# Attention and gated MLP on one core: the order of TensorE's products, by array shape, in the attention passes

## The chip, the cores and the metric

The kernel runs on one core of one Trainium2 chip. The metric is device time in microseconds (us) of one execution; lower is better. For the kernel before there are three timed runs and one profiled execution.

## What is computed

```python
scores = scale * np.matmul(q, k.transpose(0, 1, 3, 2))     # batch 4, 12 heads, 448 rows, head_dim 64
scores = cap * np.tanh(scores / cap)
scores = scores - np.max(scores, axis=-1, keepdims=True)
attn = np.exp(scores)
attn = attn / (np.sum(attn, axis=-1, keepdims=True) + 1e-09)
x = np.matmul(attn, v)                                      # laid out as (1792, 768)
h = x @ w_in                                                # w_in 768 x 2048
g = h * (1.0 / (1.0 + np.exp(-h)))
return (g @ w_out).astype(np.float32)                       # w_out 2048 x 768
```

## The kernel before, in words

The program has two stages, `attention()` and `moe()`. The change touches the first.

A head pair is two heads of one batch, one in partitions 0 to 63, the other in 64 to 127. Attention works through 24 pairs, two in a pass, so there are 12 passes. The order of all engines' work in a pass is written out by hand in the table `SLOT`: `attention()` reads its words from left to right and calls `step()` on each, and every engine keeps the order in which its instructions were recorded. In a word, `i` and `k` name the first and the second pair of the pass, the digit names a chunk of 128 keys, `r` the 64 keys that are left of 448 (of both pairs together), and `+1`, `-1`, `-2`, `-4` another pass. Two tables in `ENDS` stand in for `SLOT` in the last pass and after it.

The words, and what they record:

- `Q` (`qk`, L318; `Qr` is `qk_rem`, L330) is the scores of one chunk, keys by rows. TensorE's array is used in four quarters of 64x64: four products of 64 keys and 448 rows, which run side by side. This is one *group*; the profile shows every product twice, so a group is 8 records. It goes to one of three score tiles `s` in PSUM.
- `T` (`tanh`, L340; `Tr` is L344) is ScalarE's tanh out of the score tile into `P` in SBUF, which gives the score tile free. `E` (`exp`, L348) is the exponential in place in `P`: one over 1792 columns for chunks 0 and 1, one over 896 for chunk 2, one over 896 for the rest.
- `V` (`pv`, L380) multiplies `P` with the values `VT`: products of shape 128x64, two side by side, 4 records a group. `Vr` (`pv_rem`, L388) does so for the rest, in the 64x64 shape. All add up in one PSUM tile `o`, of which there is one; `UC` (`u_vals`, L409) copies it out on VectorE before the next pass may write it.
- `S` (`sums`, L358, L363) adds `P` up over key chunks on VectorE into `T`; `A` (`fold`, L392) adds the rest by two accumulating DMAs from GpSimd's queue; `SUM` (`pv_sum`, L402) multiplies `T` with ones (shape 128x32, one group) into a score tile, and `UT` and `N` turn the sums round, send them through the `R` DMAs and scale `U` with them.
- `L1` loads the keys and queries `QK` of pair 2s+3 and the values `VT` of the next pass, in each third pass the `VB` of the rest too; `L2` loads `QK` of pair 2s+4. There are three `QK` tiles, so each load waits for the last product that reads the tile. All these are issued by GpSimd, one after the other. `D1` and `D2` decode 64-bit weights on VectorE (`decode`), by the table `FIRST`; the last step of a weight's decoding lets GpSimd load the next raw weight into `RAW` (L603, L605), three times in the passes.
- `H` in the last two passes are six parts of the first MLP product (128x128).

So a pass has 15 groups on TensorE: seven of Q and one of Vr in the shape 64x64, six of V in 128x64, and one of SUM in 128x32.

Of the kernel before, what the change touches and what calls it, by code (L numbers as in the profile page):

```python
# [185 lines left out]
def tile_softcap_attention_swish_moe(  # L186
# [18 lines left out]
    S = NT // B  # L205
    D = DM // (2 * NP)
    KC = S // 128
# [37 lines left out]
    VT = [a1.tile([128, 2, 2 * KC * D], F32, name=f"VT{r}") for r in range(2)]  # L245
# [49 lines left out]
    def scores_tile():  # L295
        return ps_s.tile([128, 2, 512], F32, tag="s", name="s")

    def load_rem(b, eng=nc.gpsimd):
        v = vrem[b].rearrange("k (u t) d -> k u t d", t=2)
        for t in range(2):  # L300
            for e in range(2):
                eng.dma_start(out=VB[b % 2][half(t), :, e], in_=v[half(e), :, t, D * e:D * e + D])

    def load_qk(i, eng=nc.gpsimd, c0=0, c1=S + KW):
        eng.dma_start(out=QK[i % 3][:, c0:c1], in_=qkv[i, :, c0:c1])  # L305

    def load_v(s, eng=nc.gpsimd):
        for t in range(2):
            eng.dma_start(out=VT[s % 2][:, t], in_=qkv[2 * s + t, :, S + KW:])

    def qk(i, j):

        q = QK[i % 3]
        ps = scores_tile()
        for c in range(2):
            for e in range(2):
                k0 = S + 128 * j + 64 * c
                nc.tensor.matmul(  # L318
                    ps[half(c), e, 0:S], q[half(e), k0:k0 + 64], q[half(e), 0:S], start=True, stop=True
                )  # L320
        SP[i, j] = ps
# [24 lines left out]
    def exp(i, h):  # L346
        p = P[i, h]
        nc.scalar.activation(out=p, in_=p, func=AF.Exp, scale=factor(capt))  # L348

    def flat(t):  # L350
        return t.rearrange("p a s -> p (a s)")

    def sums(i, n):
# [8 lines left out]
        else:  # L362
            nc.vector.tensor_tensor(flat(T[i]), flat(T[i]), flat(p), ALU.add)  # L363

    DONE = {}

    def summed(i):
        if i // 2 not in O:
            O[i // 2] = ps_o.tile([128, 2, 512], F32, tag="o", name="o")
        n = DONE[i] = DONE.get(i, 0) + 1  # L370
        return n == 1, n == KC + 1

    def pv(i, j):

        s, t = divmod(i, 2)
        start, stop = summed(i)
        for e in range(2):
            v = VT[s % 2][:, t, D * (e * KC + j):D * (e * KC + j) + D]
            p = P[i, j // 2][:, 2 * (j % 2) + e]
            nc.tensor.matmul(O[s][half(e), t, 0:S], v, p, start=start, stop=stop)  # L380

# [8 lines left out]
    def fold(s):  # L390
        for t in range(2):
            nc.gpsimd.dma_start(out=T[2 * s + t][half(t)], in_=P[s, "r"][half(t)], accum_op=ALU.add)  # L392

    def pv_sum(s, folded=True):

        ps = scores_tile()
        for z in (1,) if folded else (0, 1):
            for t in range(2):
                for e in range(2):
                    k = 2 * e + t  # L400
                    a, p = (1 + t, P[s, "r"]) if z == 0 else (0, T[2 * s + t])
                    nc.tensor.matmul(  # L402
                        ps[32 * k:32 * k + 32, 0, 0:S], ones[:, a], p[:, e], start=(z == 0 or folded), stop=(z == 1)
                    )
        US[s] = ps

    def u_vals(s):
        U[s] = au.tile([128, 2, S], F32, tag="U", name="U", bufs=3)
        nc.vector.tensor_copy(U[s], O.pop(s)[:, :, 0:S])  # L409
# [4 lines left out]
    def u_sums(s, parts=(0, 1, 2)):  # L414
        if 0 in parts:
            UW[s] = au.tile([128, S // 32, 32], F32, tag="US", name="US", bufs=2)
            nc.vector.transpose(flat(UW[s]), US.pop(s)[:, 0, 0:S])
        if 1 in parts:
            CW[s] = au.tile([128, S // 32], F32, tag="CS", name="CS", bufs=1)
            nc.vector.reciprocal(out=CW[s], in_=UW[s][:, :, 0])  # L420
        if 2 not in parts:
            return
        u = UW.pop(s)
        nc.vector.transpose(u, CW.pop(s).unsqueeze(2).to_broadcast([128, S // 32, 32]))
        rt = flat(u)

        r = au.tile([128, 2, S], F32, tag="R", name="R", bufs=2)
        for e in range(2):
            for h in range(2):
                for c in range(2):  # L430
                    nc.sync.dma_start(
                        out=r[64 * e + 32 * h:64 * e + 32 * h + 32, c], in_=rt[64 * e + 32 * c:64 * e + 32 * c + 32]
                    )
        RB[s] = r

    def norm(s, parts=(0, 1, 2)):
        b, u = s // NU, s % NU
        cs = slice(b * S, (b + 1) * S)
        x = U[s]
        xh, xl = XH[:, 2 * u:2 * u + 2, cs], XL[:, 2 * u:2 * u + 2, cs]  # L440
        if 0 in parts:
            nc.vector.tensor_tensor(flat(x), flat(x), flat(RB.pop(s)), ALU.mult)
        if 1 in parts:
            nc.vector.tensor_copy(xh, x)
        if 2 in parts:
            nc.vector.tensor_tensor(xl, x, xh.bitcast(F32), ALU.subtract)
            if s == NS - 1:
                tail.close()
                MPOOL["acc2"] = pool(core, "acc2", 1, side="right")
# [36 lines left out]
    }  # L486

    SLOT = """
        Ti0 N0-4 Vk1-1 Ti1 Vk0-1 Sk1-1 Er-1 SUM-2 Ti2 N1-4 Vk2-1 A-1 UT0-2 Ei0 Vr-1 N2-4 Qr Ei1 UT1-2 Qk0 UC-1 L1 Tr Qk1
        Si0 Tk0 Qk2 Tk1 D1 Qi0+1 L2 Tk2 D2 Vi0 Ek0 UT2-2 Vi2 Si1 Vi1 Qi1+1 Ek1 Sk0 Qi2+1  # L490
    """.split()

    ENDS = {
        NS - 1: """
        Ti0 N0-4 Vk1-1 Ti1 Vk0-1 Sk1-1 Er-1 SUM-2 Ti2 N1-4 Vk2-1 A-1 UT0-2 Ei0 Vr-1 N2-4 Qr Ei1 UT1-2 Qk0 UC-1 Tr Qk1
        Si0 Tk0 Qk2 Tk1 D1 H0 Tk2 Vi0 Ek0 UT2-2 Vi2 Si1 Vi1 H1 Ek1 Sk0 H2
        """.split(),
        NS: """
        N0-4 Vk1-1 Vk0-1 Sk1-1 Er-1 SUM-2 N1-4 Vk2-1 Vr-1 N2-4 UC-1 H3 H4 H5 UT0-2 UT1-2 UT2-2 SUM-1 UT0-1 UT1-1 UT2-1
        """.split(),  # L500
    }

    def step(op, sh, slot):
        s = slot + sh
        if not 0 <= s < NS:
            return
        i = 2 * s + (1 if op[1:2] == "k" else 0)
        j = int(op[2]) if op[2:3].isdigit() else None
        if op == "SUM":
            pv_sum(s, s + 1 < NS)  # L510
        elif op == "UC":
            u_vals(s)
        elif op[:2] == "UT":
            u_sums(s, (j,))
        elif op[0] == "N":
            norm(s, (int(op[1]),))
        elif op[0] == "D":
            if (slot, op) in FIRST:
                decode(*FIRST[slot, op])
        elif op == "A":  # L520
            if s + 1 < NS:
                fold(s)
        elif op == "L1":
            if s + 1 < NS:
                load_qk(2 * s + 3)
                load_v(s + 1)
                if (s + 1) % NU == 0:
                    load_rem((s + 1) // NU)
        elif op == "L2":
            if s + 2 < NS:  # L530
                load_qk(2 * s + 4)
            if s < 2:
                load_w(s + 1, nc.gpsimd)
        elif op[1] == "r":
            dict(Q=qk_rem, T=tanh_rem, V=pv_rem)[op[0]](s) if op[0] != "E" else exp(s, "r")
        elif op[0] == "E":
            exp(i, j)
        else:
            dict(Q=qk, T=tanh, V=pv, S=sums)[op[0]](i, j)
        if (op, s) == ("Ti1", 0):  # L540
            setup3()
        if (op, s) == ("Ei1", 0):
            load_factors()

    def attention():
# [62 lines left out]
    def decode(m, steps):  # L608

        for step in steps:  # L610
            raw = WR[m]
            if WIDE:
                f64_bits(nc, raw.bitcast(U32).rearrange("p (n t) -> p n t", t=2), KRV, RAW[m % NBUF][:, 0:DM], step, m < 4)
            f = RAW[m % NBUF][:, 0:DM]
            if step == 4:
                if m % 6 < 3:
                    t = W02[m % 6]
                else:
                    t = MPOOL["w"].tile([128, 2 * DM], F32R, tag=f"w{m % 6}", name="w")
                WS[m] = t.rearrange("p (a n) -> p a n", a=2)  # L620
                if m < 4:
                    nc.vector.tensor_copy(WS[m][:, 0], f)
                else:
                    nc.scalar.activation(out=WS[m][:, 0], in_=f, func=AF.Copy)  # L624
            elif step == 5:
                nc.vector.tensor_tensor(WS[m][:, 1], f, WS[m][:, 0].bitcast(F32), ALU.subtract)
                if m + 3 < 2 * NF:
                    load_w(m + 3, nc.gpsimd if m < 3 else nc.sync)
# [219 lines left out]
```

## Time and profile before

| | us |
|---|---|
| median of 3 runs | 630.26 (629.03 to 631.73) |
| the profiled execution's own time | 629.94 |
| its span | 628.2 |
| first product of the MLP stage starts at | 161.17 |
| TensorE busy over the span | 619.3 |

The granted TensorE clock is 1.0 of full speed all through. The profile is read from the top: busy time by engine, then the chain of waits that ended last, then the time line of one pass. Rows name an engine (PE is TensorE, PEld its weight loads, ACT ScalarE, DVE VectorE, POOL GpSimd), a line of the kernel, the tile written and read, shapes, and a count.

### The profile page before, as it was taken

The page shows a single profiled execution, that of the slowest core. Times are in us where ns is not written, and L with a number is a line of the kernel's source. Part 1 is how long each engine was busy: PE and PEld are TensorE (multiplying, and loading weights), DVE is VectorE, ACT ScalarE, POOL GpSimd, SP SyncE. Part 2 cuts the span into 40 slices and gives each one's busy share as a digit, 9 for nine tenths or more (in the row PEclk, how much of TensorE's full clock was granted, in tenths as well). Part 3 has the DMA queues.
Part 4 walks back from the last instruction along what each step waited for, and adds up shares of the span by engine and source line. Part 5 has one row for each costly group of instructions (what it writes and reads, how often), then busy time and mean ns, then how long its engine had stood idle before and what let it go on. Part 6 is the DMA issues. An engine that isn't in the chain of part 4 may idle for free.

```text
span 628.2 us, 9065 instructions
## 1 busy us (share of the span) xinstructions
PE 619.3 (99%) x3662; PEld 478.9 (76%) x3662; DVE 420.2 (67%) x661; ACT 258.4 (41%) x333; POOL 54.7 (9%) x90
## 2 busy tenths in 40 slices
PE   7999999999999999999999999999999999999996
PEld 3333323233799989989998999899989989999996
DVE  2779888787796776756684676558556856675343
ACT  6999999997213122322322222222222223222110
POOL 2253433521000000000000000000000000000000
PEclk9999999999999999999999999999999999999999
DMA  8889998984210411201130211111111201100224
GB/s 241 236 206 206 258 206 170 247 192 69 65 45 1 152 50 51 61 40 51 52 100 12 81 60 51 51 51 51 51 50 51 101 0 54 48 0 2 101 100 156
DMA packets 18498, 59.20 MB, mean 94 GB/s; under 512 B 4592, under 2 KB 8304, under 8 KB 18448
## 3 DMA queue, kind: packets, MB, share of 16 engines
q1 hardware_dynamic: 12496, 34.32, 17.0%
q0 software_dynamic: 5952, 24.22, 16.5%
q8 instruction: 31, 0.51, 0.3%
q14 instruction: 19, 0.16, 0.1%
HBM read 42.47 MB, written 5.51 MB: 76 GB/s over the span
## 4 chain that ended last, share of the span: by engine, by line
PE 95%; DMA 3%; ACT 1%; issue 0%; DVE 0%; SPq 0%; ACTq 0%; POOLq 0%
PE s L692 37%; PE h L641 36%; PE o L380 9%; PE s L318 7%; DMA QK<-in_qkv_dram 2%; PE s L402 2%; PE o L388 2%; PE s L330 1%; PE s L641 1%; DMA capt<-in_cap_dram 1%; ACT P L340 0%; ACT P L348 0%; PE h L692 0%; SPq L305 0%; ACT P L344 0%
## 5 line engine op out<-in xcount | busy, mean ns | idle before, releaser
L641 PE MATMUL h<-XH,w 128*128 128x512 f32 (+1 forms) x756 | 217.5, 363 | 0.0
L692 PE MATMUL s<-w,gh 128*128 128x384 f32 x892 | 191.3, 335 | 0.0
L692 PEld LDWEIGHTS s<-w,gh 128*128 128x128 f32 x892 | 157.8, 188 | 2.9
L641 PEld LDWEIGHTS h<-XH,w 128*128 128x128 f32 x756 | 136.7, 188 | 22.1 <-issue 0.7
L641 PE MATMUL h<-XL,w 128*128 128x512 f32 (+1 forms) x378 | 137.5, 364 | 0.0
L656 ACT ACTIVATE gf<-h 128x512 f32<-128x512 f32 (+1 forms) x63 | 34.2, 543 | 205.1 <-PE h L641 204.8
L692 PE MATMUL s<-w,gl 128*128 128x384 f32 x446 | 113.7, 335 | 0.0
L657 DVE TENSOR_TENSOR gf<-h,gf 128x512 f32<-128x512 f32 (+1 forms) x63 | 39.2, 622 | 104.1 <-ACT gf L656 104.1
L716 DVE TENSOR_TENSOR acc<-s,acc 128x384 f32<-128x384 f32 x195 | 99.1, 550 | 8.7 <-PE s L692 8.5
L692 PEld LDWEIGHTS s<-w,gl 128*128 128x128 f32 x446 | 80.9, 188 | 0.0
L641 PEld LDWEIGHTS h<-XL,w 128*128 128x128 f32 x378 | 71.2, 188 | 10.4
L348 ACT ACTIVATE P<-P 128x896 f32<-128x896 f32 (+1 forms) x58 | 70.6, 1274 | 0.0
L667 DVE TENSOR_TENSOR gl<-gf,gh 128x512 fp32r<-128x512 f32 (+1 forms) x64 | 40.0, 625 | 38.2 <-ACT gh L663 38.2
L318 PE MATMUL s<-QK 64*64 64x448 f32 x576 | 61.9, 553 | 2.6 <-ACT P L344 1.9
L380 PE MATMUL o<-P,VT 128*64 128x448 f32 x288 | 61.8, 551 | 0.0
L663 ACT ACTIVATE gh<-gf 128x512 fp32r<-128x512 f32 (+1 forms) x64 | 37.1, 579 | 59.3 <-DVE gf L657 59.3
L340 ACT ACTIVATE P<-s 128x896 f32<-128x896 f32 x69 | 60.0, 931 | 0.6 <-PE o L380 0.5
L318 PEld LDWEIGHTS s<-QK 64*64 64x64 f32 x576 | 21.0, 135 | 39.8 <-issue 15.1
L380 PEld LDWEIGHTS o<-P,VT 128*64 128x64 f32 x288 | 17.5, 136 | 41.5 <-issue 26.6
L624 ACT ACTIVATE w<-RAW 128x768 fp32r<-128x768 f32 x28 | 23.7, 846 | 57.0 <-DVE RAW L180 50.4
L358 DVE SCALAR_TENSOR_TENSOR T<-P,epst 128x896 f32<-128x896 f32 x24 | 27.6, 1148 | 13.6 <-ACT P L348 13.6
L169 ACT ACTIVATE KRV<-RAW 128x768 f32<-128x768 f32 x28 | 25.0, 893 | 17.6 <-DVE RAW L180 13.1
(67 smaller groups left out, 376.4 us busy)
## 6 DMA issues: line engine op xcount, KB each, us to landing
RAW<-in_moe_w_in_dram SPq DMA_DIRECT2D x14, 768.0 KB, 4.3
QK<-in_qkv_dram POOLq DMA_DIRECT2D x21, 480.0 KB, 6.0
RAW<-in_moe_w_out_dram SPq DMA_DIRECT2D x13, 768.0 KB, 4.4
R<-US SPq DMA_DIRECT2D x96, 56.0 KB, 5.0
out_dram<-acc SPq DMA_DIRECT2D x13, 384.0 KB, 2.3
T<-P POOLq DMA_DIRECT2D x22, 224.0 KB, 6.0
VT<-in_qkv_dram POOLq DMA_DIRECT2D x22, 192.0 KB, 5.8
RAW<-in_moe_w_out_dram POOLq DMA_DIRECT2D x3, 768.0 KB, 7.1
```

What stands on the lines that cost most here:

```text
L318: nc.tensor.matmul(ps[half(c), e, 0:S], q[half(e), k0:k0 + 64], q[half(e), 0:S], start=True, stop=True)
L340: nc.scalar.activation(out=p, in_=SP.pop((i, j))[:, :, 0:S], func=AF.Tanh, scale=factor(sct))
L348: nc.scalar.activation(out=p, in_=p, func=AF.Exp, scale=factor(capt))
L358: nc.vector.scalar_tensor_tensor(out=flat(T[i]), in0=flat(p[:, 0:2]), scalar=epst[:, 0:1], in1=flat(p[:, 2:4]), op0=ALU.add, op1=ALU.add,)
L380: nc.tensor.matmul(O[s][half(e), t, 0:S], v, p, start=start, stop=stop)
L641: nc.tensor.matmul(ps[:, 0:n], w[:, a, kk * 128:(kk + 1) * 128], x[:, kk, t0:t0 + n], start=(kk == 0 and a == 0 and x is XH), stop=(kk == ...
L656: nc.scalar.activation(out=gf[:, 0:n], in_=ps[:, 0:n], func=AF.Sigmoid)
L657: nc.vector.tensor_tensor(gf[:, 0:n], ps[:, 0:n], gf[:, 0:n], ALU.mult)
L663: nc.scalar.activation(out=gh[:, 0:n], in_=gf[:, 0:n], func=AF.Copy)
L667: nc.vector.tensor_tensor(gl[:, 0:n], gf[:, 0:n], gh[:, 0:n].bitcast(F32), ALU.subtract)
L692: nc.tensor.matmul(pa[e][:, 0:NO2], g[a][:, ts], w[:, b, e * NO2:(e + 1) * NO2], start=(z == 0 and a == 0 and b == 0), stop=(z == G - 1 an ...
L716: nc.vector.tensor_tensor(ae, pa[e][:, 0:NO2], ae, ALU.add)
```

## The change

Three things change, all in the attention stage. The table `SLOT` and its two stand-ins are written in another order; `CHUNK = (1, 2, 0)` lets the chunk named 2 be the keys that are loaded first, named 0 and 1 the others (the same chunks are read); and two one-time set-ups hang on other words. No instruction of the passes is added or taken away.

```diff
-                k0 = S + 128 * j + 64 * c
+                k0 = S + 128 * CHUNK[j] + 64 * c
...
+    CHUNK = (1, 2, 0)
...
-            v = VT[s % 2][:, t, D * (e * KC + j):D * (e * KC + j) + D]
+            v = VT[s % 2][:, t, D * (e * KC + CHUNK[j]):D * (e * KC + CHUNK[j]) + D]
...
     SLOT = """
-        Ti0 N0-4 Vk1-1 Ti1 Vk0-1 Sk1-1 Er-1 SUM-2 Ti2 N1-4 Vk2-1 A-1 UT0-2 Ei0 Vr-1 N2-4 Qr Ei1 UT1-2 Qk0 UC-1 L1 Tr Qk1
-        Si0 Tk0 Qk2 Tk1 D1 Qi0+1 L2 Tk2 D2 Vi0 Ek0 UT2-2 Vi2 Si1 Vi1 Qi1+1 Ek1 Sk0 Qi2+1
+        Er-1 Sk0-1 Vi1-1 Ti2 Vk2-1 N0-4 Ti0 Vk1-1 Ti1 N1-4 Vk0-1 Sk1-1 Ei1 SUM-2 A-1 Ei0 Qk2 UT0-2 D1 Qr Tk2 N2-4 Vr-1 L1
+        Tr Qk0 UT1-2 Si0 Qk1 Tk0 L2 Qi2+1 UC-1 Tk1 Qi0+1 Ek1 D2 Qi1+1 Ek0 UT2-2 Vi2 Si1 Vi0
     """.split()
...
-        if (op, s) == ("Ti1", 0):
+        if (op, s) == ("Ti0", 0):
             setup3()
-        if (op, s) == ("Ei1", 0):
+        if (op, s) == ("Ei0", 0):
             load_factors()
```

The first place is TensorE in one pass in the middle of attention, before the change: L318 and L330 are the score products (64x64), L380 the values (128x64), L388 the rest (64x64), L402 the sums (128x32).

```order
L318 MATMUL s<-QK_85 64x448 x12
L318 MATMUL s<-QK_86 64x448 x4
L380 MATMUL o<-P,VT_89 64x448 x6
L318 MATMUL s<-QK_86 64x448 x8
L380 MATMUL o<-P,VT_89 64x448 x4
L402 MATMUL s<-T,ones 32x448 x4
L380 MATMUL o<-P,VT_89 64x448 x2
L388 MATMUL o<-P,VB_90 64x448 x4
L330 MATMUL s<-QK_86 64x448 x2
L330 MATMUL s<-QK_87 64x448 x2
```

The same place of the changed kernel, where two lines have been added above, so that L380, L388 and L402 are L381, L389 and L403:

```order
L318 MATMUL s<-QK_85 64x448 x8
L318 MATMUL s<-QK_86 64x448 x12
L381 MATMUL o<-P,VT_89 64x448 x12
L403 MATMUL s<-T,ones 32x448 x4
L318 MATMUL s<-QK_87 64x448 x4
L330 MATMUL s<-QK_86 64x448 x2
L330 MATMUL s<-QK_87 64x448 x2
L389 MATMUL o<-P,VB_90 64x448 x4
```

Before, the shape changes six times in a pass (into L380, L318, L380, L402, L380, L388); now three times (into L381, L403, L318). One L318 group of the second pair now stands ahead of the two L330 rows.

The second place is GpSimd's DMA queue in a pass that loads a raw weight, before the change: the fold, then `L1`, then the weight, then `L2`.

```order
L392 DMA T<-P 64x896 x2
L305 DMA QK_87<-in_qkv_dram 128x960
L309 DMA VT_89<-in_qkv_dram 128x384 x2
L603 DMA RAW_67<-in_moe_w_in_dram 128x768
L305 DMA QK_85<-in_qkv_dram 128x960
```

The same place now:

```order
L393 DMA T<-P 64x896 x2
L605 DMA RAW_67<-in_moe_w_in_dram 128x768
L305 DMA QK_87<-in_qkv_dram 128x960
L309 DMA VT_89<-in_qkv_dram 128x384 x2
L305 DMA QK_85<-in_qkv_dram 128x960
```

The raw weight has moved from between `L1` and `L2` to ahead of both. The fold keeps its place in the queue, but in the table its word `A` now stands a few words ahead of `L1`.

## Rows read from the trace of the kernel before

**Rows 1.** The page: the chain of work that ended last, by engine.
```profile
PE 95%; DMA 3%; ACT 1%; issue 0%; DVE 0%; SPq 0%; ACTq 0%; POOLq 0%
```

**Rows 2.** TensorE's time line: start, length, line, records (two for each product).
```profile
70.05 0.98 PE L388 MATMUL o<-P,VB 64*64 64x448 f32 x8
...
74.72 2.48 PE L380 MATMUL o<-P,VT 128*64 128x448 f32 x12
77.12 1.74 PE L318 MATMUL s<-QK 64*64 64x448 f32 x16
78.79 1.72 PE L380 MATMUL o<-P,VT 128*64 128x448 f32 x8
80.44 0.96 PE L402 MATMUL s<-T,ones 128*32 128x448 f32 x8
81.33 0.97 PE L380 MATMUL o<-P,VT 128*64 128x448 f32 x4
82.23 0.98 PE L388 MATMUL o<-P,VB 64*64 64x448 f32 x8
83.04 0.93 PE L330 MATMUL s<-QK 64*64 64x448 f32 x8
```

**Rows 3.** ScalarE's time line: in brackets the only idle time of a pass.
```profile
84.06 0.92 ACT L344 ACTIVATE P<-s 128x896 f32<-128x896 f32 x1 [0.73 <-PE s L330]
```

**Rows 4.** VectorE's time line: two decoding steps; then from the sums to the copy of `o`.
```profile
36.60 0.55 DVE L622 CAST w<-RAW 128x768 fp32r<-128x768 f32 x1
37.19 0.96 DVE L626 TENSOR_TENSOR w<-RAW,w 128x768 fp32r<-128x768 f32 x1
...
81.47 0.65 DVE L417 STREAM_TRANSPOSE US<-s 128x448 f32<-128x448 f32 x1 [0.94 <-PE s L402]
82.04 1.05 DVE L446 TENSOR_TENSOR XL<-U,XH 128x896 fp32r<-128x896 f32 x1
83.01 0.23 DVE L420 RECIPROCAL CS<-US 128x14 f32<-128x14 f32 x1
83.28 1.09 DVE L409 COPY U<-o 128x896 f32<-128x896 f32 x1
84.29 1.14 DVE L358 SCALAR_TENSOR_TENSOR T<-P,epst 128x896 f32<-128x896 f32 x1
```

**Rows 5.** TensorE's waits over the whole run: in total, times, longest.
```profile
PE s L318 <- ACT P L344: 1.9, 1, 1.9
...
PE s L318 <- DMA QK<-in_qkv_dram: 0.7, 1, 0.7
```

**Rows 6.** TensorE's time line around its wait for a transfer.
```profile
120.35 2.44 PE L318 MATMUL s<-QK 64*64 64x448 f32 x24
123.48 0.98 PE L318 MATMUL s<-QK 64*64 64x448 f32 x8 [0.70 <-DMA QK<-in_qkv_dram]
```

**Rows 7.** Busy time in stretches; the last two columns are DMA share and GB/s.
```profile
36.00:132.00 96.00, 95.30 (x748) 29.75 (x744) 79.77 (x100) 90.29 (x96) 40.66 (x63) 1.00 0.95 221
60.00:72.00 12.00, 12.00 (x100) 3.73 (x96) 9.91 (x13) 11.26 (x13) 4.37 (x7) 1.00 0.98 258
```

**Rows 8.** GpSimd's time line: one first load, then a pass with a raw weight.
```profile
84.27 0.60 POOL L305 DMA_DIRECT2D QK<-in_qkv_dram  x1 [2.15 <-PE s L330]
...
104.76 1.72 POOL L392 DMA_DIRECT2D T<-P  x2 [5.49 <-ACT P L348]
108.64 0.60 POOL L305 DMA_DIRECT2D QK<-in_qkv_dram  x1 [2.16 <-PE s L330]
...
114.53 0.56 POOL L305 DMA_DIRECT2D QK<-in_qkv_dram  x1 [1.13 <-DMA QK<-in_qkv_dram]
```

**Rows 9.** DMA view, 106 to 110 us: packets, and that pass's first `QK` load, us to landing.
```profile
DMA packets 133, 0.42 MB, mean 105 GB/s; under 512 B 16, under 2 KB 16, under 8 KB 133
...
QK<-in_qkv_dram POOLq DMA_DIRECT2D x1, 480.0 KB, 5.3
```

**Rows 10.** DMA view, 114.4 to 114.8 us: the second `QK` load of that pass.
```profile
QK<-in_qkv_dram POOLq DMA_DIRECT2D x1, 480.0 KB, 8.8
```

More of the change, by code (lines that the diff above doesn't have):

```diff
@@ L494, in tile_softcap_attention_swish_moe @@
         NS - 1: """
-        Ti0 N0-4 Vk1-1 Ti1 Vk0-1 Sk1-1 Er-1 SUM-2 Ti2 N1-4 Vk2-1 A-1 UT0-2 Ei0 Vr-1 N2-4 Qr Ei1 UT1-2 Qk0 UC-1 Tr Qk1
-        Si0 Tk0 Qk2 Tk1 D1 H0 Tk2 Vi0 Ek0 UT2-2 Vi2 Si1 Vi1 H1 Ek1 Sk0 H2
+        Er-1 Sk0-1 Vi1-1 Ti2 Vk2-1 N0-4 Ti0 Vk1-1 Ti1 N1-4 Vk0-1 Sk1-1 Ei1 SUM-2 A-1 Ei0 Qk2 UT0-2 D1 Qr Tk2 N2-4 Vr-1
+        Tr Qk0 UT1-2 Si0 Qk1 Tk0 H0 UC-1 Tk1 H1 Ek1 H2 Ek0 UT2-2 Vi2 Si1 Vi0
         """.split(),
         NS: """
-        N0-4 Vk1-1 Vk0-1 Sk1-1 Er-1 SUM-2 N1-4 Vk2-1 Vr-1 N2-4 UC-1 H3 H4 H5 UT0-2 UT1-2 UT2-2 SUM-1 UT0-1 UT1-1 UT2-1
+        Er-1 Sk0-1 Vi1-1 Vk2-1 N0-4 Vk1-1 N1-4 Vk0-1 Sk1-1 SUM-2 Vr-1 UT0-2 N2-4 H3 H4 H5 UC-1 SUM-1 UT1-2 UT2-2
+        UT0-1 UT1-1 UT2-1
         """.split(),
```

## The prediction

> **What bounds the kernel now.** I read the page's chain first: TensorE holds 95% of the end [rows 1]. Its waits are few: 1.9 us for ScalarE at the start and 0.7 us for a transfer [rows 5]. So what shortens TensorE's own work shortens the run, as long as nothing else comes late. The time line of a pass is next. Passes follow each other every 82.23 - 70.05 = 12.18 us, without idle time [rows 2]. ScalarE idles only 0.73 us of a pass [rows 3], so it is busy for 11.45 us. The DMA engines are busy for 95% of the passes from 36 to 132 us [rows 7]. Three resources thus lie within 6% of each other, and the reader should keep all three in view.
>
> **What a change of shape costs.** Neighbouring runs of products differ in length, which separates a group from a change [rows 2]. From 74.72 to 77.12 stand three groups of 128x64 and one change of shape, 2.40 us; from 81.33 to 82.23 one group and one change, 0.90 us. Two groups are thus 1.50 us, a group 0.75 and a change 0.15. A pass has 15 groups, 11.25 us; the other 0.93 us of 12.18 are six changes of 0.155 us each. All six stretches give 0.14 to 0.17, whichever two shapes meet: the 128x32 group, 80.44 to 81.33, leaves 0.14. Between products of different lines but one shape there is no such loss: six groups of L388, L330 and L318 and one change lie between 70.05 and 74.72, 4.67 us, so the change keeps 0.17.
>
> **What the change saves.** Three changes a pass go, 0.465 us, and a pass becomes 11.72 us. Counted over the program: the ten passes from the second to the eleventh lose three changes each, the last (with H) goes from ten to seven, the first from four to two, 35 in all. In the first, TensorE waits for ScalarE in either order (the 1.9 us [rows 5]), so I count those two as nothing. 33 x 0.155 = 5.1 us.
>
> **The wait that is there now.** The three groups from 120.35 end at 122.60, and the next starts at 123.48: 0.9 us lost on the second `QK` load of a pass that loads a raw weight [rows 6]; that load took 8.8 us to land [rows 10]. Its place in the queue changes, so I take 0.9 off here and count all lateness below.
>
> **What moves in GpSimd's queue.** The fold's two DMAs, which the queue moved slowly, at 105 GB/s [rows 9], were issued 3.88 us ahead of the first `QK` load [rows 8]. That load landed 9.2 us after the fold's issue (3.88 + 5.3 [rows 9]). Now the fold waits for the same late sum, and the load can follow on its 1.72 us of issue. If queue order rules, the load still lands 9.2 us after the fold, 7.5 us after its own issue; if the fold is out of the way, 5.3 us. The deadline: the load is issued 84.27 - 83.04 = 1.23 us after `Qr` starts [rows 2, 8], and is now needed by `Qk2`, one group ahead of the next `Qr`: 11.72 - 0.75 - 1.23 = 9.7 us (before, 10.9). An ordinary pass has 2.2 us to spare.
>
> In three passes the raw weight, 768 KB, now stands ahead of this load. At the 258 GB/s of such a stretch [rows 7] it takes 3.0 us: 7.5 + 3.0 = 10.5, 0.8 us late. **Three times 0.8 us is 2.4 us.** The lower bound is 5.3 + 3.0 = 8.3, not late, nothing. The upper bound takes the 8.8 us of the load that stood behind a raw weight [rows 10], and 2.2 us for the fold: 11.0, 1.3 us late three times, and the second load late by 0.7 us in the two of these passes that load `VB` as well: 5.3 us. I take 2.4, nearer the lower half, because a load that is late once moves the next deadline back too. That something comes late is likely: 95% of 96 us are 91 us of transfers, and the same passes will last only 96 x 11.72 / 12.18 = 92.4 us.
>
> The Trainium skill, "DMA: Bandwidth & Descriptors", section "Anatomy of one DMA — SWDGE (gpsimd) path", fits a GpSimd transfer as 2.0 us plus its bytes over 436 GB/s. By that the fold, the raw weight and the `QK` load together would be an estimated 6.0 us, the sum would have no lateness, and the time would be 623.9. The trace differs (5.3 and 8.8 us for a load of 480 KB), so the rows decide.
>
> **What costs nothing, and why.** ScalarE does the same twelve operations, 11.45 us of 11.72; its wait moves from `Tr` to `Tk0`, since `Vr` now stands between `Qr` and `Qk0`. VectorE must copy `o` before the first V product: after the sums it does a transpose, decoding, XL, a reciprocal, the T sum and the copy, 0.65 + 1.05 + 0.23 + 1.14 + 1.09 = 4.2 us, and in the worst of these passes two decoding steps, 0.55 + 0.96 = 1.5 us [rows 4]; TensorE has eight groups there, 6.0 us. The cover is 0.3 us in that pass; without it the first V product waits for the copy. `CHUNK` renames chunks and the two set-ups move by one ScalarE operation: nothing.
>
> **The sum.** 629.94 - 5.1 - 0.9 + 2.4 = 626.3 us, against the profiled execution's own 629.94, which is 0.3 below the median of 630.26.
>
> **Rivals.**
>
> *No transfer comes late.* The lower bound above: 629.94 - 5.1 - 0.9 = 623.9 us. For it speaks that an ordinary load lands 4 us ahead of its deadline; against it the 95%. Chance 0.2. The Trainium skill's fit named above, in its page on DMA, says the same.
>
> *The transfers set the pass: slower.* `Qr` frees the tile, the load refills it, `Qk2` needs it and stands ahead of the next `Qr`: a loop of 1.23 us, the landing and 0.75 us. It decides from a landing of 9.7 us in ordinary passes too. If the fold stays wholly ahead (448 KB at 105 GB/s is 4.4 us, on top of 5.3 and some 1.1 of the `R` transfers: 10.8), each of ten passes is 1.1 us late: 623.9 + 11 = 635 us. For it: every row of the fold's slowness; against: the fold is issued at least 1.72 us earlier and was already partly ahead of the load. Chance 0.08.
>
> *ScalarE sets the pass.* If its idle 0.73 us stays at the new place, the pass stays 12.18 us and only the 0.9 us go: 629.0 us. Against it: a late ScalarE finds its scores waiting, so the idle time shrinks with the pass, to 0.27 us. Chance 0.12. The Trainium skill, "TensorEngine Tiling (Array Packing)", section "PSUM Bottleneck", warns that the evacuation of PSUM can become the limit when TensorE gains; the rows here leave ScalarE 0.27 us short of that.
>
> *The loss does not hang on the shape.* If each stretch loses its 0.15 us to something else, such as a first product that waits for new data, fewer stretches would still mean fewer losses, but perhaps not three: no change, 629.9 us. Against it: six equal losses at six different meetings. Chance 0.08.
>
> **How the numbers follow.** The forecast, with lateness between 1 and 5 us, has 0.52: 625 to 629 us. A measurement of this kernel can tell 0.5%, so faster means under 627.1. The forecast gives 0.36 there and 0.16 above; the first rival adds 0.2 to faster; ScalarE and the shape rival 0.2 to no change; the transfers 0.07 to slower and 0.01 to no change. Faster 0.56, same 0.37, slower 0.07. The range goes from the first rival, 623.6, to the no-change cases, 630.0.
>
> **What would show it.** Right: passes every 11.7 us in which TensorE's time line has rows of 64, 24 and 8 records; idle time before `Qk2` (L318), put down to the DMA of `QK`, in the passes that load a raw weight, 0 to 1.3 us each; ScalarE idle about 0.3 us a pass, before a tanh of L340. Wrong: changes of another length than 0.15 us, such waits in ordinary passes, waits of L318 for ScalarE past the second pass, or of the first V row for the copy L410.

## The result and the profile after

The changed kernel takes 625.25 us (median of 4 runs, 624.82 to 625.38) against 630.47 us for the kernel before: ratio 0.9917, 95% interval 0.9895 to 0.9939. The forecast was 626.3 us, faster. The profiled execution took 625.16 us with a span of 623.3 us, 4.9 less than before. All of it lies in the attention stage: the first product of the MLP stage starts at 156.36 us instead of 161.17, 4.8 earlier.

A pass first, on TensorE's time line, against [rows 2]:

```profile
70.28 0.93 PE L389 MATMUL o<-P,VB 64*64 64x448 f32 x8
71.03 3.94 PE L318 MATMUL s<-QK 64*64 64x448 f32 x40
74.90 4.73 PE L381 MATMUL o<-P,VT 128*64 128x448 f32 x24
79.56 0.96 PE L403 MATMUL s<-T,ones 128*32 128x448 f32 x8
80.45 0.98 PE L318 MATMUL s<-QK 64*64 64x448 f32 x8
81.25 0.93 PE L330 MATMUL s<-QK 64*64 64x448 f32 x8
82.00 0.93 PE L389 MATMUL o<-P,VB 64*64 64x448 f32 x8
```

From L389 to L389 it is 82.00 - 70.28 = 11.72 us, without idle time, instead of 12.18. From 79.56 to 81.25 there are two groups and the change from 128x32 to 64x64, 0.89 and 0.80 us. From 81.25 to 82.00 the line changes (L330 to L389) and the shape does not: 0.75 us, a group and nothing else.

TensorE's waits over the run, against [rows 5], and the place of the one for a transfer, against [rows 6]:

```profile
PE s L318 <- ACT P L340: 2.1, 1, 2.1
...
PE s L318 <- DMA QK<-in_qkv_dram: 0.8, 2, 0.5
```

```profile
117.93 1.68 PE L318 MATMUL s<-QK 64*64 64x448 f32 x16
120.11 2.49 PE L318 MATMUL s<-QK 64*64 64x448 f32 x24 [0.50 <-DMA QK<-in_qkv_dram]
```

Two groups from 117.93 would end at 119.43; the next starts at 120.11. So 0.7 us were lost on the second load of keys that the ninth pass issues; `Qi2` of the next pass waits for it. (Below, a late load is named by the pass that issues it.) The other wait of that row is 0.30 us at 7.67 us, in the first pass. No first load of a pass (`L1`) was late. The DMA views at the issue of three first loads (an ordinary pass, the fifth and the ninth with a raw weight) and of that second load, against [rows 9, 10]:

```profile
QK<-in_qkv_dram POOLq DMA_DIRECT2D x1, 480.0 KB, 4.3
...
QK<-in_qkv_dram POOLq DMA_DIRECT2D x1, 480.0 KB, 6.6
...
QK<-in_qkv_dram POOLq DMA_DIRECT2D x1, 480.0 KB, 5.6
...
QK<-in_qkv_dram POOLq DMA_DIRECT2D x1, 480.0 KB, 8.5
```

GpSimd's time line shows why the first loads are early, against [rows 8]:

```profile
65.59 0.87 POOL L393 DMA_DIRECT2D T<-P  x1 [3.73 <-ACT P L348]
68.60 0.82 POOL L393 DMA_DIRECT2D T<-P  x1 [2.14 <-DVE T L363]
70.76 0.60 POOL L305 DMA_DIRECT2D QK<-in_qkv_dram  x1 [1.34 <-PE s L330]
```

The fold has come apart. Its first transfer, of the pass's first pair, goes out 5.2 us ahead of the load, only the second 2.2 us ahead. Before, both went out together, 3.9 us ahead.

ScalarE has the little idle time that was forecast (0.27 us), before the tanh of L340; the stretch of this row is the same pass:

```profile
72.03 1.73 ACT L340 ACTIVATE P<-s 128x896 f32<-128x896 f32 x2 [0.28 <-PE s L318]
```

The start is what no part of the forecast had. TensorE's wait for ScalarE in the first pass, in the kernel before and in the changed one:

```profile
12.95 1.78 PE L318 MATMUL s<-QK 64*64 64x448 f32 x16 [1.89 <-ACT P L344]
...
12.28 4.93 PE L318 MATMUL s<-QK 64*64 64x448 f32 x32 [2.12 <-ACT P L340]
```

In the changed kernel, busy time in stretches of 1 us, the third column from the right being the granted clock, and TensorE's weight loads of half a group each:

```profile
12.00:13.00 1.00, 0.72 (x8) 0.21 (x8) 0.97 (x2) 1.00 (x3) 0.00 (x0) 0.76 0.88 333
13.00:14.00 1.00, 1.00 (x12) 0.46 (x8) 0.74 (x1) 0.89 (x3) 0.00 (x0) 0.50 0.94 375
14.00:15.00 1.00, 1.00 (x8) 0.27 (x4) 0.00 (x0) 1.00 (x2) 0.82 (x2) 0.50 0.43 166
```

```profile
13.63 0.27 PEld L318 LDWEIGHTS s<-QK 64*64 64x64 f32 x4 [0.36 <-issue]
14.38 0.27 PEld L318 LDWEIGHTS s<-QK 64*64 64x64 f32 x4 [0.48 <-issue]
15.13 0.27 PEld L318 LDWEIGHTS s<-QK 64*64 64x64 f32 x4 [0.48 <-issue]
```

After the 2.12 us in which TensorE waited for ScalarE, the granted clock was 0.50, the 1.2 GHz level, and half groups came every 0.75 us, not every 0.375. In the profiled execution before, TensorE waited 1.89 us at that place [rows 5] and the granted clock stayed at 1.0. The kernel before has other executions too: of its 22 runs beside e1 to e4, the 12 with a mean granted clock of 0.998 or more have a median span of 628.0 us, the 10 below it 630.6; where the clock fell in those is not on record.

### The profile page after: what moved, and what is told of

Same layout as the page of the kernel before. It is cut to its first block, busy times and chain, and to the rows that moved or that the text cites. A ratio compares the mean times of both kernels' runs of the same rounds, so it can differ in the third digit from the quotient of the medians.

```text
span 623.3 us, 9043 instructions
## 1 busy us (share of the span) xinstructions
PE 614.1 (99%) x3662; PEld 482.3 (77%) x3662; DVE 419.1 (67%) x661; ACT 258.6 (41%) x333; POOL 54.2 (9%) x90
## 4 chain that ended last, share of the span: by engine, by line
PE 96%; DMA 2%; SPq 1%; ACT 0%; issue 0%; DVE 0%; ACTq 0%
PE s L694 37%; PE h L643 37%; PE o L381 8%; PE s L318 8%; PE s L403 2%; DMA QK<-in_qkv_dram 1%; PE o L389 1%; PE s L330 1%; PE s L643 1%; DMA VB<-in_vrem_dram 0%; SPq L302 0%; ACT P L348 0%; SPq L305 0%; PE h L694 0%; SPq L309 0%
## 5 line engine op out<-in xcount | busy, mean ns | idle before, releaser
L348 ACT ACTIVATE P<-P 128x896 f32<-128x896 f32 (+1 forms) x58 | 68.7, 1256 | 0.0
L318 PE MATMUL s<-QK 64*64 64x448 f32 x576 | 62.2, 560 | 2.9 <-ACT P L340 2.1
L340 ACT ACTIVATE P<-s 128x896 f32<-128x896 f32 x69 | 60.1, 924 | 4.0 <-PE s L318 2.8
L381 PE MATMUL o<-P,VT 128*64 128x448 f32 x288 | 56.8, 543 | 0.0
L318 PEld LDWEIGHTS s<-QK 64*64 64x64 f32 x576 | 21.1, 136 | 41.2 <-issue 16.0
L381 PEld LDWEIGHTS o<-P,VT 128*64 128x64 f32 x288 | 19.6, 137 | 36.0 <-issue 31.5
```

The lines of the kernel that those rows point to most:

```text
L318: nc.tensor.matmul(ps[half(c), e, 0:S], q[half(e), k0:k0 + 64], q[half(e), 0:S], start=True, stop=True)
L340: nc.scalar.activation(out=p, in_=SP.pop((i, j))[:, :, 0:S], func=AF.Tanh, scale=factor(sct))
```

## The experiments

Times below are spans of the profiled execution (before 628.2, changed 623.3), since most effects are smaller than what the runs' medians can tell; the medians are given too. Each trace is one execution, and its start and its late loads are its own. Each ratio is to the kernel before.

### One change of shape more: e1_sums_among_values

```diff
-        Er-1 Sk0-1 Vi1-1 Ti2 Vk2-1 N0-4 Ti0 Vk1-1 Ti1 N1-4 Vk0-1 Sk1-1 Ei1 SUM-2 A-1 Ei0 Qk2 ...
+        Er-1 Sk0-1 Vi1-1 Ti2 Vk2-1 N0-4 Ti0 Vk1-1 SUM-2 Ti1 N1-4 Vk0-1 Sk1-1 Ei1 A-1 Ei0 Qk2 ...
```

> The changed kernel with the group of sums (128x32) put back among the value products (128x64): the same 15 groups a pass, four changes of shape instead of three, in the ten passes that have sums. If each change of shape costs 0.155 us, a pass becomes 11.72 + 0.155 = 11.88 us, and the span grows from 623.3 to 624.9 us. If the gain came from the transfers or from ScalarE's new order, and not from the shapes, a pass stays 11.72 us and the span 623.3 us.

Median 626.03 us, ratio 0.9923 (0.9894 to 0.9951), span 624.5 us. TensorE's time line, from L389 to L389:

```profile
71.23 0.93 PE L389 MATMUL o<-P,VB 64*64 64x448 f32 x8
71.98 3.94 PE L318 MATMUL s<-QK 64*64 64x448 f32 x40
75.85 3.98 PE L381 MATMUL o<-P,VT 128*64 128x448 f32 x20
79.76 0.96 PE L403 MATMUL s<-T,ones 128*32 128x448 f32 x8
80.65 0.97 PE L381 MATMUL o<-P,VT 128*64 128x448 f32 x4
...
83.11 0.93 PE L389 MATMUL o<-P,VB 64*64 64x448 f32 x8
```

The pass is 83.11 - 71.23 = 11.88 us, as the price of a change says. The span grew by 1.2 us and not 1.6, because this trace has no late load in its passes (0.7 us less; e10, further down, shows that the late load can be missing without any edit), while its start was 0.35 us later (first L389 at 23.71 instead of 23.36).

### One change less, in the kernel before: e2_before_one_change_less

```diff
-        ... Vk0-1 Sk1-1 Er-1 SUM-2 Ti2 N1-4 Vk2-1 A-1 ...
+        ... Vk0-1 Sk1-1 Er-1 Vk2-1 SUM-2 Ti2 N1-4 A-1 ...
```

> The kernel before with one word moved: the last value group goes ahead of the sums, so that a pass has five changes of shape instead of six; the order of ScalarE's work and of the transfers stays. If each change costs 0.155 us: a pass of 12.18 - 0.155 = 12.03 us, and over ten passes 1.6 us less, span 626.6 us. If the gain needs the new order of ScalarE or of the loads: 12.18 us and 628.2 us.

Median 628.91 us, ratio 0.9953 (0.9928 to 0.9978), span 627.3 us. The time line, from L388 to L388:

```profile
70.64 0.98 PE L388 MATMUL o<-P,VB 64*64 64x448 f32 x8
...
79.38 2.48 PE L380 MATMUL o<-P,VT 128*64 128x448 f32 x12
81.78 0.96 PE L402 MATMUL s<-T,ones 128*32 128x448 f32 x8
82.67 0.98 PE L388 MATMUL o<-P,VB 64*64 64x448 f32 x8
```

82.67 - 70.64 = 12.03 us. With three, four, five and six changes a pass, the passes are thus 11.72, 11.88, 12.03 and 12.18 us: a straight line of 0.155 us a change, in either order of the other engines. The span fell by 0.9 us and not by the expected 1.6: the start of this execution was 1.1 us later (TensorE waited 2.4 us for ScalarE, and the first L388 came at 22.25 instead of 21.14), and the wait for the late load was 0.16 us instead of 0.70.

### Both folds late: e3_both_folds_late

```diff
     def fold(s):
-        for t in range(2):
+        for t in (1, 0):
```

> The changed kernel with the fold's two transfers issued in the opposite order, so that the first of them waits for the later sum and both stand right ahead of the first load of keys. Theory: the load lands early in the changed kernel (4.0 to 4.5 us after its issue in ordinary passes) because half of the fold is issued 5 us ahead of it and is out of the way. Then the load will now land 6.5 to 7.0 us after its issue, and in the passes with a raw weight TensorE waits for it, 0 to 0.8 us each: span 623.3 to 625.5 us. Rival, that the order of these transfers does not matter: landing stays at 4.0 to 4.5 us and the span at 623.3 us.

Median 631.4 us, ratio 1.0022 (1.0003 to 1.0041), span 628.3 us: the whole gain is gone, 5.0 us where the theory allowed at most 2.2. The DMA views of the first loads, three ordinary passes (issued at 71.38, 83.10 and 95.05 us):

```profile
QK<-in_qkv_dram POOLq DMA_DIRECT2D x1, 480.0 KB, 6.9
...
QK<-in_qkv_dram POOLq DMA_DIRECT2D x1, 480.0 KB, 6.7
...
QK<-in_qkv_dram POOLq DMA_DIRECT2D x1, 480.0 KB, 6.0
```

The landing went from 4.0 to 4.5 us up to 6.0 to 6.9, as the theory says and the rival does not. What the theory had too small is the lateness around the passes with a raw weight. TensorE's waits, and its time line with the loads of the ninth pass:

```profile
PE s L318 <- DMA QK<-in_qkv_dram: 5.9, 4, 2.2
```

```profile
117.22 0.98 PE L318 MATMUL s<-QK 64*64 64x448 f32 x8 [0.69 <-DMA QK<-in_qkv_dram]
...
123.38 3.69 PE L318 MATMUL s<-QK 64*64 64x448 f32 x24 [2.17 <-DMA QK<-in_qkv_dram]
127.01 5.17 PE L381 MATMUL o<-P,VT 128*64 128x448 f32 x24
```

Of the four waits one lies in the first pass (1.24 us at 8.29 us). The others are for the second load of the third pass (1.81 us at 49.66 us) and for both loads of the ninth. Behind the last, of 2.17 us, TensorE ran at a lower granted clock again (0.63 from 124 to 126 us): the three groups took 3.69 us instead of 2.49, the six value groups 5.17 instead of 4.73. From L389 to L389, behind the second one, four passes are longer than 11.72 us, by 7.1 us together. The span shows 5.0, since the start of this execution was 1.4 us earlier (second L389 at 33.69 instead of 35.10) and the changed kernel lost 0.7 us to its own late load.

### The raw weight last: e4_raw_weight_last

```diff
-        ... UT0-2 D1 Qr Tk2 N2-4 Vr-1 L1
-        Tr Qk0 UT1-2 Si0 Qk1 Tk0 L2 Qi2+1 UC-1 Tk1 ...
+        ... UT0-2 Qr Tk2 N2-4 Vr-1 L1
+        Tr Qk0 UT1-2 Si0 Qk1 Tk0 L2 Qi2+1 UC-1 D1 Tk1 ...
```

> The changed kernel with the decoding step D1 moved behind both loads of keys, so that a raw weight stands behind them in GpSimd's queue instead of ahead. Theory: the wait of 0.5 us for the second load of keys in the ninth pass (0.7 us lost) comes from the raw weight ahead of it, so it goes: span 622.6 us. Rival: the transfers of that pass are as many as before and only the next load is late instead, by 0.5 to 0.9 us: span 623.3 to 623.5 us.

Median 625.06 us, ratio 0.991 (0.9878 to 0.9942), span 623.2 us. Each theory was half right. The wait for the ninth pass's load is gone, as the theory says. With the raw weight behind it that load took 4.3 us instead of 8.5:

```profile
110.83 0.58 POOL L305 DMA_DIRECT2D QK<-in_qkv_dram  x1
111.42 0.55 POOL L607 DMA_DIRECT2D RAW<-in_moe_w_out_dram  x1
...
QK<-in_qkv_dram POOLq DMA_DIRECT2D x1, 480.0 KB, 4.3
```

The second loads of the third and fifth pass, which also had a raw weight ahead, went from 5.8 to 3.9 us and from 8.5 to 6.2. But the span is the rival's, since a load of the sixth pass is late instead (0.76 us):

```profile
82.62 1.68 PE L318 MATMUL s<-QK 64*64 64x448 f32 x16
84.83 2.49 PE L318 MATMUL s<-QK 64*64 64x448 f32 x24 [0.52 <-DMA QK<-in_qkv_dram]
```

It is again the second load of a pass that loads `VB`, here without a raw weight in the same pass. That pointed to `VB`, which e8 tries. The two passes from 34.61 to 58.42 us are also 0.2 us longer each, for a reason that is not shown; the start of this execution was 0.5 us earlier.

### The start kept busy: e5_start_kept_busy

```diff
-    def warm():
+    def warm(n=3):
...
-        nc.vector.memset(z, 0.0)
+        if n == 3:
+            nc.vector.memset(z, 0.0)
...
-        for _ in range(3):
+        for _ in range(n):
...
+        if (op, s) == ("Qk0", 0):
+            warm(4)
```

> The changed kernel with four products of zeros (128x128, 256 columns) put into TensorE's idle time in the first pass, where it waits 2.1 us for ScalarE; they write a tile that the first value product overwrites. Theory: the clock that was granted at half speed from 12.5 to 15.9 us fell because of that idle time, and made four groups take 0.75 us for each half instead of 0.375. Then the clock stays at 1.0, the first value product starts at 15.8 to 16.0 us instead of 17.14, and the span is 1.0 to 1.3 us shorter, 622.0 to 622.3 us. Rival: ScalarE, which starts late and has a full pass of work, sets the start; then the clock may stay up, but TensorE waits for ScalarE some passes later, and the span stays at 623.3 us, or grows by 0.2 us for the products.

Median 624.77 us, ratio 0.9917 (0.9895 to 0.9939), span 623.0 us. The granted clock stayed at 1.00 in the stretches where it was 0.50, so the theory is right on the clock:

```profile
13.00:14.00 1.00, 1.00 (x16) 0.28 (x15) 0.79 (x1) 1.00 (x3) 0.33 (x1) 1.00 0.90 361
14.00:15.00 1.00, 1.00 (x16) 0.34 (x16) 0.00 (x0) 1.00 (x2) 0.74 (x2) 1.00 0.71 229
```

The first value product started at 15.64 us instead of 17.14. But of these 1.5 us, 0.5 went back in the second pass, to ScalarE, and 0.7 at the ninth pass's load, where TensorE came to the late load earlier and waited longer: it went on at 119.75 us, against 120.11. (The wait at that place is put down to ScalarE in this trace; the load landed 0.1 us before its end.) Both theories were half right.

### Value groups earlier: e7_values_earlier

```diff
     ENDS = {
+        0: """
+        Ti2 Ti0 Ti1 Ei1 Ei0 Qk2 D1 Qr Tk2 L1 Tr Qk0 Vi2 Vi0 Vi1 Si0 Qk1 Tk0 L2 Qi2+1 Tk1 Qi0+1 Ek1 D2 Qi1+1 Ek0 Si1
+        """.split(),
+        1: [op for op in SLOT if op != "Vi1-1"],
```

> The changed kernel with an order of its own in the first pass: the three value groups of the first pair stand ahead of the score groups that wait for ScalarE, at the price of two changes of shape (0.3 us). Theory, that TensorE's idle time and slow clock set the start: three groups (2.25 us) move into the 2.1 us of idle time, so the span is 1.0 to 1.9 us shorter, 621.4 to 622.3 us. Rival, that ScalarE sets the start: it has lost only 0.6 us there, waiting for a value group, so at most 0.6 us less the 0.3 us of the two changes is gained: 623.0 us, or nothing.

Median 625.04 us, ratio 0.9923 (0.9901 to 0.9945), span 623.3 us: nothing gained. The work moved into the gap, the granted clock stayed at 1.0, and the gap came back a pass later, as a wait of 1.55 us for ScalarE at 24.33 us: ScalarE sets the start, as the rival says. What was gained there (second L389 at 34.77 instead of 35.10) went to the late load: TensorE waited 0.84 us for it instead of 0.50 and went on at 120.11 us, as in the changed kernel.

### VB behind the keys, alone and with the busy start: e8_rest_behind_keys, e9_both

```diff
                 load_v(s + 1)
-                if (s + 1) % NU == 0:
-                    load_rem((s + 1) // NU)
...
                 load_qk(2 * s + 4)
+                if (s + 1) % NU == 0:
+                    load_rem((s + 1) // NU)
```

> The changed kernel with the four loads of the values' rest (VB, in each third pass) moved behind the second load of keys; they are needed a pass later only. Theory: in the ninth pass the second load of keys lands 0.5 us late because it is issued 2.4 us later and stands behind the four loads and the raw weight; then it is issued at about 109.0 us instead of 111.43 and lands before 119.4 us, no product waits for a transfer, and the span is 0.7 us shorter, 622.6 us. Rival: its landing is set by the raw weight and by the total of that pass's transfers; then the wait stays, span 623.3 us.

> The changed kernel with the zero products of the start and with the four loads behind the second load of keys. Theory: the start gains 1.0 us net (1.5 us at the first pass, 0.5 us given back to ScalarE in the second), which was lost again to the late load of the ninth pass, where TensorE waited for 1.18 us; without that wait the gain stays: span 621.5 to 621.9 us. Rival, that transfers set the pace up to the ninth pass: the wait comes back at another load and the span is 622.6 to 623.0 us.

> The changed kernel once more, beside the two others on the same chip: span 623.3 us, ratio to the kernel before 0.992.

| kernel, all on one chip | median us | ratio to before (interval) | span us |
|---|---|---|---|
| e8, VB last | 623.97 | 0.9885 (0.986 to 0.991) | 622.2 |
| e9, VB last and busy start | 623.98 | 0.9882 (0.9857 to 0.9907) | 622.5 |
| e10, the change as it is | 624.75 | 0.9906 (0.9878 to 0.9934) | 623.0 |

In e8 the second load of the ninth pass is issued at 108.16 us, 3.3 us sooner. It takes even longer, 10.3 us, and lands at 118.46, but TensorE runs through:

```profile
QK<-in_qkv_dram POOLq DMA_DIRECT2D x1, 480.0 KB, 10.3
```

```profile
117.47 3.94 PE L318 MATMUL s<-QK 64*64 64x448 f32 x40
121.34 4.73 PE L381 MATMUL o<-P,VT 128*64 128x448 f32 x24
```

So an earlier issue brings the landing forward: to 118.46 us and, in e9, 118.07, against 119.35 to 119.95 in the four traces with 11.72 us passes and the change's order of issue (the change, e5, e7, e10). TensorE came to it at 118.97 and 119.29. But e10, the change without any edit, has no late load in its passes either. Its load landed at 119.35 us and TensorE came to it at 119.83:

```profile
118.33 3.94 PE L318 MATMUL s<-QK 64*64 64x448 f32 x40
```

Half a microsecond thus decides whether the load is late, and the changed kernel shows both. Neither version is told from the change by the intervals, which overlap. The medians are 0.8 us lower, but in the traces the 0.8 us between e10 and e8 are not the wait: they lie in the start (second L389 at 35.51 and at 34.65 us), which the move of `VB` does not touch. What that move is worth in time is not shown.

e9 is no better than e8, missed its 621.5 to 621.9 us, and the wait at another load that its rival expected did not come either. In e8 TensorE started as fast without the zero products: its idle time fell into two parts, 1.29 us for a transfer at 9.10 us and 1.33 us for ScalarE, and the granted clock stayed at 1.0.

The starts differ from run to run by when the first transfers land, so kernels are best compared from ScalarE's first tanh. It starts at 6.62 us before, at 5.95 in the changed kernel, 6.59 in e8 and 6.91 in e9. From there to the second L389 it is 28.06 or 28.07 us in e3, e4, e5, e8 and e9, whose granted clock stayed at 1.0 in the start, 29.15 in the changed kernel and 29.52 in e10. ScalarE has no idle time over this stretch in e8. From the first tanh to the MLP stage it is 161.17 - 6.62 = 154.55 us before, 150.41 after, 148.61 in e8 and 148.61 in e9 (155.20 and 155.52 us). Without its own late load, 0.88 us, the kernel before would be at 153.67: e8 and e9, which have neither a late load behind the first pass nor a slow clock, show by difference a gain of the shapes of 5.06 us.

## Why the prediction was right

**The price of a change of shape: right.** 0.155 us was read from six stretches of one pass; four kernels with three to six changes lie on that line.

**Its sum: right.** 33 x 0.155 = 5.1 us, against the 5.06 above, a difference of single traces. A pass was to be 11.72 us and is 11.72.

**The lateness: right in kind, wrong in size and place.** The step that failed is "the fold waits for the same late sum, and the load can follow on its 1.72 us of issue". Only the second of the fold's two transfers waits for the late sum; the first goes out 3 us earlier. The first loads of the passes therefore landed after 3.7 to 6.6 us, and not after 7.5 to 10.5. Instead of 2.4 us on three first loads, 0.7 us were lost on one second load, the case that the forecast had named only in its upper bound. e3 makes the forecast's assumption true, with both transfers right ahead of the load, and its passes lose 7.1 us: the forecast's 2.4 would have been too little, and so would its upper bound of 5.3. Even there only one first load was late; most of the loss is on second loads of the two passes that load `VB` as well.

**The start: missed.** The two changes saved there were counted as nothing, because TensorE waits for ScalarE. In the profiled execution of the changed kernel the start took 29.15 - 28.06 = 1.1 us longer than in e8 (its second L389 is at 35.10, 29.15 us after the first tanh; in e8, at 34.65, 28.06 us after its own), through the granted clock of 0.50. That belongs to the execution and not to the order, which is the same in e8.

**The account.** Shapes -5.06, the old late load -0.88, the new one +0.73, the slow start +1.1, and the first tanh 0.67 us earlier in this execution: -4.8 us, which is what the start of the MLP stage shows; the sum closes because its terms are differences of the same traces. The forecast's time came out near partly by luck: too much lateness stood in place of a slow start.

**The rivals.** That no transfer comes late did not hold in the profiled execution of the change, but it did, behind the first pass, in e10, the same kernel once more; so this rival is not excluded, and half a microsecond decides between the two. Its 623.9 us lies 0.9 below e10's median, 624.75. That ScalarE sets the pass is excluded by its idle 0.28 us, but it sets the start (the 28.06 us of five kernels). That the loss does not hang on the shape is excluded by e1, e2 and the 0.75 us between lines of one shape. That transfers set the pace of ordinary passes did not come, not even in e3, where most passes stay at 11.72 us; but one swap in a loop of two transfers was enough there to lose the gain.

**The Trainium skill.** The fit of "DMA: Bandwidth & Descriptors", section "Anatomy of one DMA — SWDGE (gpsimd) path", 2.0 us plus the bytes over 436 GB/s, gives an estimate of 3.1 us for a load of keys. The runs show 3.6 us (e4) to 10.3 us (e8) for that load. Most of the loads under 4.0 us, the nearest to the fit, are in the changed order, with half the fold out of the way and no raw weight ahead.

## What to carry to other kernels

Where products of several array shapes alternate, price a change of shape from the gaps between runs of groups in one pass, and count changes, not runs: here the saving was linear from six changes to three. Before such a reordering is called free, write down for every transfer the issue, what stands ahead of it in its queue and the product that needs it; with DMA engines busy 95% (before) and 93% (the changed kernel) of 36 to 132 us, which of two DMAs goes first was worth as much as the whole change. Profile the same kernel twice before a wait of half a microsecond is put down to an edit. Compare executions from the first instruction that follows the first landing, since that instruction came anywhere from 5.63 to 6.91 us.

## What was not expected of the hardware

The granted clock of TensorE fell to the 1.2 GHz level after waits of 2.12 us (the changed kernel), 2.24 (e10), 2.42 (e1 and e2) and 2.17 (e3's ninth pass). It stayed at the 2.4 GHz level after waits of 1.89 us (before), 1.81 (e3, at 49.66 us), 1.54 (e4) and 1.33 (e8), and in e5 and e9, where zero products stood in the gap. At 0.50 half a group took 0.75 us instead of 0.375. Where the start kept its clock without zero products in e3, e4 and e8, TensorE's idle time in the first pass was in two parts, the first for a late transfer (1.24, 2.06 and 1.29 us) and the second for ScalarE (1.18, 1.54 and 1.33).

The second load of keys in a pass with a raw weight takes long: 8.5 us in the changed kernel and 10.3 in e8, against 5.8 to 5.9 for the second load of two ordinary passes of the changed kernel and 4.0 for a first load. e4 shows what the raw weight ahead has to do with it: behind both loads instead of ahead, it left the same load at 4.3 us. Why the load in e8, issued earlier, took longer still was not tried.
